# Strassen's algorithm for the down projection of three of four token tiles, in an attention and gated feed-forward kernel

## The chip, the cores and the metric

The kernel runs on one core of a Trainium2 chip. Its time is the device time of one execution in microseconds; the number given for a kernel is the median over several executions. A profiled execution has a time of its own and a span, from its first to its last instruction, that is a little shorter.

The engines are named as in the profile: PE (TensorE, matrix products into PSUM, the accumulation memory), PEld (PE's weight loads), DVE (VectorE), ACT (ScalarE), POOL (GpSimd, which can't read PSUM) and SP (SyncE, which issues the DMAs here). Each engine works through its own queue strictly in order.

## The reference

For x of 2048 tokens and D = 512, with 32 heads of 16 and a window of 256 keys:

```python
xn  = layernorm(x)
q, k, v = heads(xn @ wqkv)                       # 32 heads of 16
p   = softmax(mask(q @ k.T * 16 ** -0.5))        # causal, 256 keys back
s   = (p @ v) @ wo
h   = silu(xn @ w1) * (xn @ w3)                  # F = 1792
g   = silu(h @ w2)                               # the down projection
out = x + s * g
```

Everything is float32 at the interface. The down projection multiplies h (2048 x 1792) by w2 (1792 x 512).

## The kernel before

**Precision.** Operands of the large products are split into two float16 parts, hi and lo, and a product is three passes: hi x hi, hi x lo, lo x hi. A cast on ACT makes hi (`slot<-slot` on line 947 for h), and a subtraction makes lo: on POOL, by `halves` (line 325), which does every 512 columns as two instructions of 256.

**Tiling.** Tokens are worked on in NT = 4 tiles of TW = 512. Attention for a tile goes by 4 groups of 8 heads and 2 halves of a group, so there are 32 `units`. In a unit, `pass2` makes scores (line 717), adds masks on DVE (line 724), takes the exponential on ACT (line 727: four per unit in the first tile, five in the others, 152 in all) and multiplies by the values (line 745); `pass1` finds the maxima two units ahead (lines 637 and 651). Scores have two PSUM buffers. `normalise` ends a group of heads: the sums of the exponentials go by DMA through `dd`, `dr`, `de` to `rb`, POOL multiplies `on` by `rb`, ACT copies to hi (line 799), and POOL subtracts for lo. These are the operands of the output projection, `total`.

**Feed-forward.** F is cut into FB = 14 blocks of 128. `gate_up(t, f)` makes the gate and up products of a block (24 passes of 512 columns, line 918), tanh on ACT (line 933), two products on DVE (lines 937 and 942), then hi and lo of h. `down(t, k, b)` multiplies for one of four groups of blocks (`GROUPS`: 4, 4, 3 and 3 blocks) and one of four blocks `b` of 128 tokens: h is the stationary operand and w2 the moving one, 512 columns wide, three passes a block (line 968). A group's sum is brought out of PSUM with its scale, `down_scale[k]`, by ACT for the first group (line 987, tiles after the first) and by DVE for the others (line 992), which adds to an accumulator `ACC[t, b]`. `total(t, b)` takes tanh of it, multiplies O by wo (line 1019), and combines (line 1023); the last block of the last tile goes by columns (`total_by_columns`, 256 wide, line 1048). These dense products alternate between two PSUM banks, `m0` and `m1`.

**Weights.** In the first tile `measure`, `measure_down` and their `cut` scale and split w1, w3 and w2; the split forms are stored to DRAM (`dW1`, `dW2`) and loaded again by `load` and `load_down` in the other tiles. wo is cut at the start of the second tile.

**Order.** PE's order is written out by the program. `feed_forward` lists the dense pieces with costs in passes; `spread` puts each unit's share of them between the batches of attention, so that every unit is of like length; `later(n, f)` issues f n steps on. What is left of the dense list when attention ends (84 passes are kept back, `KEEP`) and the last tile's `total` follow at the end without attention. For ACT, DVE, POOL and SP a list scheduler orders the instructions by when it takes them to be ready; `urgent` raises priority. The order is fixed when the kernel is built.

**Slots.** Most tiles of 2 KB a partition come from a ring of SLOTS = 40 slots (`take`, `give`), taken in the order in which they were given back.

## Time and profile before

| | us |
|---|---|
| median of 3 executions | 824.92 (824.75 to 825.98) |
| the profiled execution | 823.93 |
| its span | 822.1 |
| PE busy in it | 802.3 |
| DVE, ACT, POOL busy | 633.5, 389.4, 205.9 |

A group's row reads: line, engine, operation, result<-operands, their shape, xcount | busy us, mean ns of one | us that the engine was idle just before them, and what ended most of that. Matrix passes are pipelined: one has a modelled length of 379 ns at 512 columns while the next starts after 216, so lengths from start to start are read from rows that merge several. A row of the chain reads: start us, us, what. A row of waits reads: who waited for whom, us in total, times, longest. A row of a timeline reads: start us, us, engine, line, operation, and in brackets the idle time before it.

### The profile page before, as it was taken

The page shows a single profiled execution, that of the slowest core. Times are in us where ns is not written, and L with a number is a line of the kernel's source. Part 1 is how long each engine was busy: PE and PEld are TensorE (multiplying, and loading weights), DVE is VectorE, ACT ScalarE, POOL GpSimd, SP SyncE. Part 2 cuts the span into 40 slices and gives each one's busy share as a digit, 9 for nine tenths or more (in the row PEclk, how much of TensorE's full clock was granted, in tenths as well). Part 3 has the DMA queues.
Part 4 walks back from the last instruction along what each step waited for, and adds up shares of the span by engine and source line. Part 5 has one row for each costly group of instructions (what it writes and reads, how often), then busy time and mean ns, then how long its engine had stood idle before and what let it go on. Part 6 is the DMA issues. An engine that isn't in the chain of part 4 may idle for free. (4 is left out here: it accounts for less than half of the span.)

```text
span 822.1 us, 22902 instructions
## 1 busy us (share of the span) xinstructions
PE 802.3 (98%) x8924; PEld 380.1 (46%) x8924; DVE 633.5 (77%) x2021; ACT 389.4 (47%) x562; POOL 205.9 (25%) x355
## 2 busy tenths in 40 slices
PE   8999999999999999999999999999999999999998
PEld 4444444444444444444445444444444444444444
DVE  8787788888787588878878876877777787776435
ACT  6889785645345344243343444442433344432511
POOL 2237274342203113021211112120202022030301
PEclk9999999999999999999999999999999999999999
DMA  9987656157442444544434334534434343332101
GB/s 283 251 252 236 208 176 203 63 148 242 126 134 78 120 131 126 153 124 134 136 94 131 99 89 144 136 121 121 129 82 143 105 112 116 108 121 86 52 22 53
DMA packets 95326, 110.66 MB, mean 135 GB/s; under 512 B 17200, under 2 KB 60528, under 8 KB 95216
## 3 DMA queue, kind: packets, MB, share of 16 engines
q1 hardware_dynamic: 94928, 108.67, 45.3%
q8 instruction: 70, 1.15, 0.6%
q10 hardware_dynamic: 288, 0.52, 0.2%
q14 instruction: 40, 0.33, 0.1%
HBM read 76.28 MB, written 28.57 MB: 128 GB/s over the span
## 5 line engine op out<-in xcount | busy, mean ns | idle before, releaser
L325 POOL TENSOR_TENSOR slot<-slot,slot 128x256 f16<-128x256 f32 (+1 forms) x228 | 151.5, 691 | 518.5 <-ACT slot L947 391.9
L918 PE MATMUL m<-XH,slot 128*128 128x512 f16 x896 | 267.3, 380 | 3.1 <-DVE slot L937 1.7
L727 ACT ACTIVATE pt<-s,es 128x1024 f32<-128x1024 f32 x152 | 167.7, 1113 | 194.4 <-DVE s L724 192.5
L918 PEld LDWEIGHTS <-slot 128*128 128x128 f16 x1344 | 125.1, 98 | 158.1 <-issue 14.0
L918 PE MATMUL m<-XL,slot 128*128 128x512 f16 x448 | 169.8, 379 | 0.0
L968 PE MATMUL m<-slot,slot 128*128 128x512 f16 x672 | 156.6, 380 | 1.8 <-DVE slot L594 0.7
L724 DVE TENSOR_TENSOR s<-s,MK 128x256 f32<-128x256 f32 (+2 forms) x280 | 118.4, 435 | 49.5 <-PE s L717 47.1
L651 DVE CUSTOM_DVE_ANT_0 junk<-s,MW 128x320 bf16<-128x320 f32 x276 | 134.1, 486 | 24.3 <-PE s L637 15.8
L968 PEld LDWEIGHTS <-slot 128*128 128x128 f16 x672 | 61.9, 98 | 80.4 <-issue 9.9
L651 DVE CUSTOM_DVE_ANT_0 junk<-po,MW 128x320 bf16<-128x320 f32 x172 | 83.6, 486 | 5.1 <-DVE mt L676 0.3
L745 PE MATMUL po<-pt,V 64*32 64x320 f32 (+4 forms) x2880 | 77.2, 342 | 0.0
L947 ACT CAST slot<-slot 128x512 f16<-128x512 f32 x56 | 34.5, 617 | 73.4 <-DVE slot L942 68.7
L933 ACT ACTIVATE slot<-m,sgs 128x512 f32<-128x512 f32 x56 | 38.3, 684 | 56.8 <-PE m L918 56.8
L745 PEld LDWEIGHTS po<-pt,V 64*32 64x32 f32 x2880 | 51.0, 106 | 21.4 <-issue 0.8
L717 PE MATMUL s<-qa,KA 50*64 50x320 f16 (+3 forms) x1472 | 58.2, 259 | 1.2 <-ACT pt L727 0.6
L937 DVE SCALAR_TENSOR_TENSOR slot<-slot,m 128x512 f32<-128x512 f32 x56 | 38.3, 685 | 23.4 <-ACT slot L933 23.2
L717 PEld LDWEIGHTS <-KA 50*64 50x64 f16 x1472 | 30.2, 105 | 55.6 <-issue 34.0
L637 PE MATMUL s<-KA,qa 48*64 48x320 f16 (+3 forms) x824 | 45.4, 294 | 2.9 <-ACT pt L727 1.6
L942 DVE SCALAR_TENSOR_TENSOR slot<-m,slot 128x512 f32<-128x512 f32 x56 | 38.5, 688 | 10.6 <-PE m L918 10.1
L992 DVE SCALAR_TENSOR_TENSOR slot<-m,dsc,slot 128x512 f32<-128x512 f32 x48 | 35.9, 748 | 13.4 <-PE m L968 13.1
L581 PE MATMUL m<-XH,whi 128*128 128x512 f16 x120 | 44.7, 381 | 1.1 <-DVE slot L937 0.7
L581 PE MATMUL m<-XL,whi 128*128 128x512 f16 x120 | 44.5, 379 | 0.0
(162 smaller groups left out, 875.2 us busy)
## 6 DMA issues: line engine op xcount, KB each, us to landing
slot<-dW SPq DMA_DIRECT2D x126, 256.0 KB
slot<-in_B_w_dram SPq DMA_DIRECT2D x42, 256.0 KB
dW<-slot SPq DMA_DIRECT2D x42, 256.0 KB
slot<-in_A_x_dram SPq DMA_DIRECT2D x30, 256.0 KB
KA<-dK SPq DMA_DIRECT2D x24, 288.0 KB
qa<-dQ SPq DMA_DIRECT2D x32, 192.0 KB
dQ<-slot SPq DMA_DIRECT2D x16, 256.0 KB
dK<-slot SPq DMA_DIRECT2D x16, 256.0 KB
```

Source lines behind the costliest of these rows:

```text
L325: op(out[:, c], a[:, c], b[:, c])
L581: nc.tensor.matmul(cell["pp"], a[:, k, c, :], b[:, c, :], start=(c, i) == parts[0][0], stop=(c, i) == parts[-1][-1])
L637: nc.tensor.matmul(s[c:c + w, r, :n], qa[rows, 2 * p + a, ii * P + c:ii * P + c + w], ka[rows, 2 * p + a, e - n:e], start=True, stop=True)
L651: lasts["maximum"] = nc.vector.tensor_tensor_reduce(out=junk[:, :n], in0=s[:, r, :n], in1=mask, scale=1.0, scalar=NEG, op0=ALU.add, op1=AL ...
L717: nc.tensor.matmul(s[64 * h:64 * h + 64, r, o:o + 64 * n], ka[rows, 2 * p + a, 64 * (m + 4):64 * (m + 5)], qa[rows, 2 * p + a, 64 * (m + k ...
L724: nc.vector.tensor_add(v, v, MK[:, kind, of:of + n, :].unsqueeze(1).to_broadcast([P, 2 * len(which), n, 64]))
L727: nc.scalar.activation(pt, s, AF.Exp, scale=es)
L745: nc.tensor.matmul(cell["po"][32 * i:32 * i + 32, h, 64 * (m + k):64 * (m + k + n)], V[64 * h:64 * h + 64, (4 * t + m // 2) % VB, hd * VW: ...
L918: nc.tensor.matmul(cell[k], w[:, (a * NC + c) * P:(a * NC + c + 1) * P], b[:, c, :], start=c == 0 and i == 0, stop=c == NC - 1 and i == 2)
L933: nc.scalar.activation(sg, cell[0], AF.Tanh, scale=sg_scale[:, f:f + 1])
L942: lasts["emptied"] = nc.vector.scalar_tensor_tensor(sg, cell[1], 0.5 * HS / (WS * XS)**2, sg, op0=ALU.mult, op1=ALU.mult)
L968: nc.tensor.matmul(ps, hh[:, a * TW + b * P:a * TW + (b + 1) * P], w[:, c * D:(c + 1) * D], start=f == f0 and i == 0, stop=f == f1 - 1 and ...
```

## The change

In the first tile nothing but where things go changes: `down` is as before, and the split w2 isn't stored. In the second to fourth tile the down projection goes by Strassen's algorithm in Winograd's form. The 14 blocks of F are taken as 7 pairs, an even and an odd block. The even and odd block and the even and odd 128 tokens make four blocks of h; the two blocks of w2 and the left and right 256 columns of D make four blocks of w2. Seven products of sums of these, each 256 columns wide, take the place of eight, and each is again three passes. The pairs are in two parts (`FOLDS`: 4 and 3 pairs), so that a product is summed over 4 or 3 pairs in PSUM, twice for the two halves of its tokens.

- `fold_weights(j)`, in the second tile, after its blocks 1 to 7: loads a pair of rows of w2 again, scales them on ACT (one scale for all, from `fold_scales`), makes four sums on POOL, casts all four tiles on ACT, subtracts on POOL, and stores seven operands to DRAM.
- `fold_first` and `fold_second`, after an even and an odd block: the same for h, with four sums on POOL.
- `folds`, `load_fold`, `fold_down_piece`: the loads (two products ahead) and the products, in the order `SEVEN`; the first part is brought out of PSUM by ACT, the second added by DVE.
- `unfold`: 14 additions of 256 columns on POOL turn the seven results into the four accumulators.
- 47 slots instead of 40 and a smaller scratch for DMA descriptors; the last unit's `negate` at once; the last tile's output blocks in the order 1, 3, 0, 2.

```diff
-SLOTS = 40
+SLOTS = 47
+FOLDS = ((0, 4), (4, 7))
+SEVEN = (0, 1, 3, 4, 5, 6, 2)
...
-    dW2 = dram.tile([FB, P, 2 * D], F16, name="dW2")
+    dW2 = dram.tile([7, P, FB // 2, D], F16, name="dW2")
...
-                later(2, negate)
+                later(2, negate) if (t, g, p) != units[-1] else negate()
...
+    def fold_weights(j):
+
+        raws = [take(F32) for _ in range(2)]
+        for i, raw in enumerate(raws):
+            nc.sync.dma_start(raw, w2[(2 * j + i) * P:(2 * j + i + 1) * P, :])
+        e, o = raws
+        l, r = slice(0, 256), slice(256, 512)
+        sub = nc.gpsimd.tensor_sub
+        cell = {}
+
+        def sums():
+            assert folded
+            for i, raw in enumerate(raws):
+                nc.scalar.activation(raw, raw, AF.Copy, scale=fold_w[:, 2 * j + i:2 * j + i + 1])
+            cell["z"] = z, y = [take(F32) for _ in range(2)]
+            pool_parts(sub, (z[:, l], e[:, r], e[:, l]), (z[:, r], o[:, r], z[:, l]),
+                       (y[:, l], o[:, r], e[:, r]), (y[:, r], o[:, l], z[:, r]))
+
+        def cut(raw, n, which):
+
+            a = take(F16)
+            nc.scalar.copy(a[:, 0:n], raw[:, 0:n])
+            for c in range(0, n, 256):
+                sub(a[:, n + c:n + c + 256], raw[:, c:c + 256], a[:, c:c + 256])
+            give(raw, after=4)
...
+        later(4, sums)
+        later(6, lambda: cut(e, 256, (0,)))
+        later(7, lambda: cut(o, 512, (1, 2)))
+        later(9, lambda: cut(cell["z"][0], 512, (4, 5)))
+        later(11, lambda: cut(cell["z"][1], 512, (6, 3)))
...
+    def fold_second(t, j):
...
+        nc.gpsimd.tensor_add(z[:, 0], ee[:, 1], oo[:, 1])
+        sub(z[:, 1], z[:, 0], ee[:, 0])
+        sub(y[:, 0], ee[:, 0], ee[:, 1])
+        sub(y[:, 1], oo[:, 0], z[:, 1])
+        cut(o, oo, (1, 3), (e,))
+        later(1, lambda: cut(sums[0], z, (4, 5)))
+        later(2, lambda: cut(sums[1], y, (6, 2)))
...
+    def fold_down_piece(t, k, i):
...
+            for j in range(j0, j1):
+                made, lo, at = AS[t, j, i]
+                wj = w[(j - j0) // 2][:, (j - j0) % 2 * D:]
+                for n, (a, b) in enumerate(((0, 0), (0, 1), (1, 0))):
+                    f = at + a * lo + c * P
+                    nc.tensor.matmul(ps, made[:, f:f + P], wj[:, 256 * b:256 * b + 256],
+                                     start=j == j0 and n == 0, stop=j == j1 - 1 and n == 2)
...
+            if k == 0:
+                QS7[t, i] = take(F32)
+                with urgent():
+                    nc.scalar.activation(QS7[t, i], ps, AF.Copy, scale=fold_down)
+                return
+            q = QS7[t, i]
+            with urgent():
+                lasts["emptied"] = nc.vector.scalar_tensor_tensor(q, ps, fold_down, q, op0=ALU.mult, op1=ALU.add)
+            if i != SEVEN[-1]:
+                return
+            unfold(t)
...
+    def unfold(t):
...
+        halves(add, q[5], q[5], q[0])
+        halves(add, q[6], q[6], q[5])
+        into(1, 0, q[6], q[3])
+        into(1, 1, q[6], q[4])
+        into(0, 0, q[0], q[1])
+        halves(add, q[5], q[5], q[4])
+        into(0, 1, q[5], q[2])
...
+                    if t == 1 and 1 <= f <= FB // 2:
+                        pieces.append((0, lambda f=f: fold_weights(f - 1)))
...
+                if f == 0 and t > 1:
+                    pieces += soon
...
+                for k, (j0, j1) in enumerate(FOLDS):
+                    if t and f == 2 * j1 - 1:
+                        soon, late = folds(t, k)
+                        if k == 0 or t == NT - 1:
+                            pieces += soon
...
-    for b in range(4):
-        if b < 2:
-            residual(NT - 1, b + 2)
-        if b < 3:
-            run(total(NT - 1, b))
-    total_by_columns(NT - 1, 3)
+    for n, b in enumerate((1, 3, 0)):
+        if n < 2:
+            residual(NT - 1, 2 * n)
+        run(total(NT - 1, b))
+    total_by_columns(NT - 1, 2)
...
-    nc = _bacc.Bacc("TRN2", target_bir_lowering=False, num_devices=1)
+    nc = _bacc.Bacc("TRN2", target_bir_lowering=False, num_devices=1, dynamic_dma_scratch_size=1024)
```

The products of a part follow the gate and up products of the next block, as the groups did before; those of a tile's second part fall into the next tile's first block, and in the last tile they come at the end.

More of the change, by code (lines that the diff above doesn't have):

```diff
@@ L859, in tile_block, with load_down @@
     NORMS = {}
[L861 to L865 removed]
+    def load_down(f):
         RAW2[f] = raw = take(F32)
@@ new lines, in fold_second, with cut @@
+    def fold_second(t, j):
+        e, o = (HH.pop((t, 2 * j + i)) for i in range(2))
+        ee, oo = by_parity(e), by_parity(o)
+        sub = nc.gpsimd.tensor_sub
+        sums = [take(F32) for _ in range(2)]
+        z, y = (a.rearrange("p (e c q) -> p e c q", c=2, e=2) for a in sums)
+        def cut(raw, view, which, give_too=()):
+            made = take(F16)
+            hi, lo = (made[:, 512 * k:512 * k + 512].rearrange("p (e c q) -> p e c q", e=2, c=2) for k in range(2))
+            nc.scalar.copy(hi, view)
+            for k in range(2):
+                sub(lo[:, k], view[:, k], hi[:, k])
+            for k, i in enumerate(which):
+                operand(t, j, i, made, 512, 256 * k)
+            give(raw, *give_too, after=4)
+        nc.gpsimd.tensor_add(z[:, 0], ee[:, 1], oo[:, 1])
[5 more added lines that the diff above has]
+        later(2, lambda: cut(sums[1], y, (6, 2)))
@@ new lines, in unfold, with into @@
+    def unfold(t):
+        q = [QS7.pop((t, i)) for i in range(7)]
+        add = nc.gpsimd.tensor_add
+        for b in range(4):
+            ACC[t, b] = take(F32)
+        def into(e, d, x, y):
+            for c in range(2):
+                h = slice(256 * c, 256 * c + 256)
+                add(ACC[t, 2 * c + e][:, 256 * d:256 * d + 256], x[:, h], y[:, h])
+        halves(add, q[5], q[5], q[0])
[5 more added lines that the diff above has]
+        into(0, 1, q[5], q[2])
+        give(*q, after=6)
+        summed.update((t, b) for b in range(4))
@@ L953, in tile_block, with folds @@
+    def folds(t, k):
+        loads = [(0, lambda i=i: load_fold(t, k, i)) for i in SEVEN]
+        pieces = []
+        for n, i in enumerate(SEVEN):
+            if n + 2 < 7:
+                pieces.append(loads[n + 2])
+            pieces += fold_down_piece(t, k, i)
+        return loads[:2], pieces
     ACC = {}
@@ L970, in part @@
                 if b == 3:
-                    give(hh)
-                    if t == 0:
-                        def store(f=f, w=w):
-                            nc.sync.dma_start(dW2[f], w)
-                            give(w, after=3)
-                        later(4, store)
-                    else:
-                        give(w)
+                    give(hh, w)
             if fs[-1] < f1 - 1:
@@ L1318, in tile_block @@
             later(1, lambda k=k: fetch(*tiles[k]))
-    for b in range(2):
+    for b in (1, 3):
         residual(NT - 1, b)
```

90 lines of the change are left out of this document (80 added, 10 removed).

## The prediction

> **What bounds the kernel now.** I read the page's shares first, then the groups by line with the shapes kept apart, the waits of PE, and last the end of the span in order of time.
>
> ```profile
> span 822.1 us, 22902 instructions
> PE 802.3 (98%) x8924; PEld 380.1 (46%) x8924; DVE 633.5 (77%) x2021; ACT 389.4 (47%) x562; POOL 205.9 (25%) x355
> PE   8999999999999999999999999999999999999998
> POOL 2237274342203113021211112120202022030301
> PEclk9999999999999999999999999999999999999999
> ```
>
> PE is busy nearly everywhere at full clock; no other engine reaches 80%. A busy PE could still hide stalls, so I look at what one pass costs from start to start and at what PE waits for.
>
> ```profile
> PE s L670 <- DVE NM L664: 1.8, 3, 1.1
> PE m L918 <- DVE slot L937: 1.7, 3, 0.8
> PE s L637 <- ACT pt L727: 1.6, 4, 0.7
> ```
>
> ```profile
> 808.12 7.77 PE m L1019 x36
> 815.89 2.63 PE m L1048 x24
> ```
>
> The longest sum of PE's waits on one cause is 1.8 us, so time taken from PE's own work comes off the span as long as nobody else becomes late. From the chain: 36 passes of 512 columns take 7.77 us, 0.2158 us each, and 24 passes of 256 columns 2.63 us, 0.1096 us each. A pass of half the width costs half.
>
> **The change, part by part.**
>
> *PE.* Tiles two to four lose 3 x 14 x 4 x 3 = 504 passes of 512 columns (of the 672 below) and gain 3 tiles x 7 products x 7 pairs of blocks x 2 halves x 3 terms = 882 passes of 256.
>
> ```profile
> L968 PE MATMUL m<-slot,slot 128*128 128x512 f16 x672 | 156.6, 380 | 1.8 <-DVE slot L594 0.7 <-DVE slot L942 0.5 <-POOL slot L325 0.2
> L1048 PE MATMUL m<-slot,slot 128*128 128x256 f16 x24 | 2.8, 272 | 0.0
> ```
>
> 504 x 0.2158 = 108.8 us go, 882 x 0.1096 = 96.7 us come: **-12.1 us**. The second row has a fresh weight load before every half-width pass, as the new products have, so the price includes it.
>
> *Work for POOL.* It replaces the two casts' differences of a pair of blocks (4 instructions of 256 columns) by 11, for 21 pairs; adds 11 for each of 7 pairs of rows of w2 in the second tile; and 14 for each tile's sums at the end. 292 instructions of 128x256 become 558.
>
> ```profile
> L325 POOL TENSOR_TENSOR slot<-slot,slot 128x256 f16<-128x256 f32 x204 | 134.0, 685 | 468.8 <-ACT slot L947 391.9 <-ACT slot L329 52.2 <-DMA slot<-in_B_w_dram 7.3
> L325 POOL TENSOR_TENSOR on<-on,rb 128x256 f32<-128x256 f32 x32 | 22.7, 732 | 62.6 <-DMA rb<-de 62.6
> L325 POOL TENSOR_TENSOR slot<-on,slot 128x256 f16<-128x256 f32 x32 | 20.8, 672 | 14.6 <-ACT slot L799 14.6
> L325 POOL TENSOR_TENSOR slot<-slot,slot 128x256 f32<-128x256 f32 x24 | 17.4, 747 | 49.7 <-DVE slot L1023 41.8 <-issue 7.9
> ```
>
> Over the whole span this is about 558 x 0.70 = 391 us, under half of it, and would hide. It isn't spread evenly. The built order of the changed kernel has a stretch in the second tile in which w2 is combined, its first four pairs are combined, and wo is cut, all at once. Take two marks that both kernels share, the exponentials, which ScalarE takes in the same order: between the 31st and the 45th of the 152, POOL must do 110 instructions (73 to f16, 37 to f32), the last of them before the 45th, because ScalarE's queue holds a copy of POOL's result ahead of it; the first of the 110 needs a copy queued behind the 31st. Before, these two exponentials stand here:
>
> ```profile
> 237.34 1.11 ACT L727 ACTIVATE pt<-s,es 128x1024 f32<-128x1024 f32 x1 [2.37 <-DVE s L724]
> 238.35 0.68 ACT L933 ACTIVATE slot<-m,sgs 128x512 f32<-128x512 f32 x1
> ...
> 306.60 1.11 ACT L727 ACTIVATE pt<-s,es 128x1024 f32<-128x1024 f32 x1 [0.55 <-DVE s L724]
> ```
>
> ```profile
> 239.00:306.60 67.60, 67.18 (x806) 32.22 (x805) 50.56 (x166) 31.91 (x43) 15.37 (x23) 1.00 0.40 113
> ```
>
> The window row (PE, PEld, DVE, ACT, POOL busy, clock, DMA share, GB/s) shows POOL with 23 instructions and 15.4 us in these 68 us. From 239.0 to 305.3 (306.6 less the copy and a hand-over) there are 66.3 us; the work is 73 x 0.685 + 37 x 0.747 = 77.6 us. So POOL is 11.3 us late at the 45th exponential, and late already at the 41st. Behind a late copy on ScalarE stand the exponentials and the tanh of gate blocks; behind the tanh, the products on VectorE; behind these PE's banks. What slack has an exponential? 14 of them in 69.3 us is 4.95 us each; the mask additions and the exponential take 2 x 0.43 + 1.11 of it.
>
> ```profile
> L724 DVE TENSOR_TENSOR s<-s,MK 128x256 f32<-128x256 f32 x224 | 92.3, 427 | 47.1 <-PE s L717 45.4 <-PE s L670 1.0
> L947 ACT CAST slot<-slot 128x512 f16<-128x512 f32 x56 | 34.5, 617 | 73.4 <-DVE slot L942 68.7 <-issue 2.2 <-DMA on<-os 1.9
> L328 ACT ACTIVATE slot<-slot,sw 128x512 f32<-128x512 f32 x14 | 9.8, 720 | 3.5 <-DVE sw L894 3.5
> L987 ACT ACTIVATE slot<-m,dsc 128x512 f32<-128x512 f32 x12 | 8.2, 685 | 8.9 <-PE m L968 8.9
> L992 DVE SCALAR_TENSOR_TENSOR slot<-m,dsc,slot 128x512 f32<-128x512 f32 x48 | 35.9, 748 | 13.4 <-PE m L968 13.1
> ```
>
> About 2.5 us are left over before PE wants the score bank again, so PE loses about 9. ScalarE itself has 81 instructions there instead of 43, roughly 13 x 1.11 + 68 x 0.61 = 56 of the 66 us, so two nearly full queues wait for each other; I add 1. **+10 us**, estimate from these rows; bounds 0 (POOL catches up) and 18 (POOL begins one exponential later, 4 us, and stands for the DMA of rb as long as before on average, 62.6/16 = 3.9 us).
>
> The GPSIMD Engine Reference of the Trainium skill (section 3.1) gives 2.6 cycles per element at 1.2 GHz for two-input elementwise work, 0.555 us for 256 columns without dispatch, as an estimate. By it the 110 would take 61 us, POOL would be in time, and the sum below would be 821.5. The rows of 0.685 and 0.747 stand against it.
>
> *Drains and casts.* In each tile 12 drains on VectorE (0.748) become 7, and 4 on ScalarE (0.685) become 7; the pairs get four casts instead of two, one of half width. VectorE gains 15 x 0.75 = 11 us of idle time, worth nothing while PE has the span. ScalarE at 47% covers its part, except in the stretch above.
>
> *DMA and SP's queue.* 42 loads of dW2 become 84 (half products, 256 or 128 KB), 14 stores become 49 of 128 KB, and w2 is read a second time (14 x 256 KB). In the stretch this adds 6.4 + 3.7 = 10.1 MB to 113 GB/s x 80 us = 9 MB: the DMA share goes from 0.40 to about 0.85, still under full. On SP a store that waits for a late POOL holds back the gate weights behind it; these are issued two blocks ahead, some 18 us, which covers 11. Price 0; if the lag passed 18 us, its excess.
>
> *Slots, scratch, the last unit's negation, the order of the residuals.* Space and order; two VectorE instructions of under 0.4 us move earlier. Nothing.
>
> *The end.* Here is the old one:
>
> ```profile
> 799.55 8.56 PE L968 MATMUL m<-slot,slot 128*128 128x512 f16 x36
> 807.95 7.93 PE L1019 MATMUL m<-slot,slot 128*128 128x512 f16 x36
> ...
> 808.49 0.74 DVE L992 SCALAR_TENSOR_TENSOR slot<-m,dsc,slot 128x512 f32<-128x512 f32 x1
> ...
> 807.75 0.60 ACT L799 CAST slot<-on 128x512 f16<-128x512 f32 x1
> ...
> 802.43 1.42 POOL L325 TENSOR_TENSOR on<-on,rb 128x256 f32<-128x256 f32 x2
> 808.43 1.30 POOL L325 TENSOR_TENSOR slot<-on,slot 128x256 f16<-128x256 f32 x2 [4.58 <-ACT slot L799]
> ```
>
> The last head group's output is normalised (on x rb), copied and cut for wo, just in time for the first block of L1019. In the built order of the changed kernel POOL has on x rb behind all 14 sums of the last tile, and its copy on ScalarE stands behind the four tanh that wait for these sums. Call E the moment PE ends the last product. A drain ends 1.28 us after its last pass (807.95 to 809.23); the product before the last ends at E - 1.96 (18 x 0.109), its drain at E - 0.7. Then 10 sums, 10 x 0.72 = 7.2: E + 6.5; on x rb 1.42: E + 7.9; copy 0.6 and hand-overs: E + 8.6; the first difference 0.65: E + 9.3. PE comes to these operands after 9 of 12 passes, at E + 1.94, and ends the block near E + 9.5 instead of E + 2.6: **+6.9 us**. What follows (three more blocks, last drain, store) shifts as it is. PE then stood still for 6.7 us. The only start from rest in this trace is the first:
>
> ```profile
> L1216 PE MATMUL m<-onesb 128*128 128x512 bf16 x10 | 4.2, 598 | 1.0 <-DVE onesb L189 1.0
> ...
> L1216 PE MATMUL m<-onesb 128*128 128x512 bf16 x16 | 3.8, 392 | 0.0
> ```
>
> (first 1 to 5 us, then 5 to 8 us): 10 passes in the first 4 us where 10 x 0.216 would do, 1.8 us lost. I take **+1.8** after the pause; bounds 0 and 1.8.
>
> **Sum.** 822.1 - 12.1 + 10 + 6.9 + 1.8 = 828.7 us span. The profiled execution took 823.93, 1.8 more than its span, and lies 1.0 under the median of 824.92: 831.5 us.
>
> **The rivals.**
>
> *POOL keeps pace in the second tile* (ends on the other side). It decides at 0.625 us for one POOL instruction (66.3 + 2.5 us over 110), or if PE reaches the score banks later than I think. For it: POOL was idle for three quarters of that stretch before, and VectorE's work, beside which these rows were taken, gets less. Against it: no row is under 0.67. Time 831.5 - 10 = 821.5.
>
> *Two full queues block each other.* POOL waits for copies that stand behind exponentials that wait for PE that waits for ScalarE: the upper bound, 18 instead of 10: 839.5. For it: ScalarE's 56 of 66 us. Against: POOL's order was laid down with its load in it.
>
> *The whole gain arrives:* no lag, and on x rb is in time after all: 822.1 - 12.1 + 2.8 = 812.8. Against it: the order of an engine's queue isn't a matter of speed.
>
> *Half-width passes don't cost half,* because each carries a weight load (98 ns each) that no longer fits behind it: 882 x (0.1096 + 0.098) against 504 x (0.2158 + 0.098), +25 us, 850 or more. Against it: the 24 passes of 0.1096 us carry such loads too. TensorE: Matmul & The Clock Gate of the Trainium skill (section Back-to-back issue gap) has a figure that points the same way, 81 ns a pass at 128 columns and 131 at 512 in a stream with weight loads; by it the products would cost, as an estimate, at least 882 x 0.081 = 71 us against 504 x 0.131 = 66. This trace disagrees: its passes of 512 columns take 0.2158 us.
>
> ```profile
> L968 PEld LDWEIGHTS <-slot 128*128 128x128 f16 x672 | 61.9, 98 | 80.4 <-issue 9.9
> ```
>
> **How the numbers follow.** Forecast 0.46 (its own range 826 to 836), blocked queues 0.25, POOL in pace 0.20, whole gain 0.07, dear passes 0.02. Within 0.2% (1.6 us, about what can be told from no change) falls a quarter of POOL in pace and a little of the forecast's low end: 0.06. Faster 0.15 + 0.07 = 0.22, slower 0.72. The range 819 to 843 leaves out the whole gain, the dear passes, the best of POOL in pace and the worst of the blocked queues, less than 0.2 together.
>
> **What would show it.** Right: in the products' row, 882 passes of 256 columns near 0.11 us apart; between the 31st and 45th exponential POOL busy almost without a break, the distance of the two 78 to 85 us instead of 69, ScalarE's idle time there put down to POOL; at the end PE standing 6 to 7 us within the first output block, released by POOL, and then some passes 0.43 us apart. Wrong: the two exponentials under 71 us apart; PE's pause at the end under 3 us; or a new wait elsewhere, for instance PE for a load of dW2 (two products ahead, in the last tile 1.96 us each) or POOL's 10.5 us of sums holding up on x rb at the start of the third and fourth tile.

## The result and the profile after

| | before | changed |
|---|---|---|
| median of 6 executions each, us | 825.08 (824.72 to 826.38) | 891.23 (888.39 to 895.36) |
| the profiled execution, its span | 823.93, 822.1 | 890.93, 889.2 |

The changed kernel takes 1.080 times as long (95% interval 1.0776 to 1.0828): 66 us slower, where the prediction had 6.6 us and at most 18.

The page of the changed kernel: span, busy time by engine, then PE, POOL and PE's granted clock in the 40 slices of the span (22 us each).

```profile
span 889.2 us, 24220 instructions
PE 812.9 (91%) x9302; PEld 424.7 (48%) x9302; DVE 629.3 (71%) x2013; ACT 434.3 (49%) x655; POOL 384.1 (43%) x621
PE   8999988999889669999999999999999998989995
POOL 2257353524278786113351635310434453441653
PEclk9999999999989779999999999999999998999997
```

No engine is full: PE fell from 98% to 91%, and POOL, with nearly twice its old time, is at 43%. PE's digits are lowest in the 14th and 15th slice (the second tile) and in the last one; fainter losses are in the 6th, 7th, 11th, 12th, 34th and 36th. PE's longest waits, and those of ScalarE (ACT) that the new work makes:

```profile
PE s L719 <- ACT pt L729: 18.6, 8, 5.8
PE m L978 <- DVE slot L997: 13.6, 5, 7.4
PE s L639 <- ACT pt L729: 10.8, 10, 2.7
PE m L1212 <- ACT slot L801: 7.3, 1, 7.3
```

```profile
ACT slot L801 <- POOL on L327: 36.6, 13, 6.7
ACT slot L1055 <- POOL slot L1063: 22.0, 20, 2.1
ACT slot L1206 <- POOL slot L1132: 19.2, 3, 12.3
ACT slot L1055 <- POOL slot L1065: 10.1, 16, 0.7
```

L729 is the exponential, L719 and L639 the score products that need its PSUM bank, L978 the gate and up products, L1212 the output projection. L1055 is a cast of a pair of blocks of h, L1062 to L1065 are POOL's four sums before it, L925 the sums of w2, L1206 the tanh ahead of `total`, L1132 sums of `unfold`. PE waits for exponentials, ScalarE for POOL; in the kernel before, PE's waits on one cause came to 1.8 us at most. Of the three waits at L1206, one of 4.6 us is at the start of the fourth tile, and the other two, 14.6 us, come after the last exponential.

The 152 exponentials are the same in every kernel here, in the same order, so their starts (rows of L729 in the timeline) say where time is lost. In us later than in the kernel before:

| up to exponential | 23 | 31 | 45 | 61 | 109 | 139 | 152 | PE's end |
|---|---|---|---|---|---|---|---|---|
| changed kernel | 5.8 | 7.5 | 37.1 | 39.2 | 43.2 | 61.0 | 59.0 | 66.9 |

So 29.6 us are lost in the second tile between the 31st and the 45th, 17.8 late in attention (109 to 139), 7.9 at the end, 7.5 before the 31st. In the second tile exponentials stand whose scores are ready: from the end of their masks to their start, the 14 from the 32nd to the 45th stand at least 36.1 us in all, against 3.1 before. The second tile in windows of 20 us (busy us and instructions of PE, PEld, DVE, ACT and POOL, then clock, DMA share, GB/s):

```profile
260.00:280.00 20.00, 16.40 (x147) 7.46 (x147) 12.81 (x40) 11.83 (x19) 17.86 (x28) 0.83 0.43 122
280.00:300.00 20.00, 12.62 (x163) 5.60 (x161) 9.51 (x28) 9.49 (x14) 16.11 (x25) 0.81 0.50 137
300.00:320.00 20.00, 14.23 (x103) 6.06 (x102) 9.51 (x32) 8.85 (x14) 14.14 (x23) 0.76 0.54 155
320.00:340.00 20.00, 16.67 (x193) 8.41 (x192) 10.87 (x32) 10.07 (x15) 12.43 (x19) 0.91 0.76 226
```

POOL is busy for 60.5 of these 80 us, ScalarE for 40, PE for 60: they take turns at waiting. The chain of work that ended last shows how, in order of time:

```profile
301.74 0.59 SPq L769
...
303.01 0.54 SPq L770
...
303.64 2.67 DMA slot<-in_B_w_dram
...
306.34 0.73 ACT slot L940
...
307.14 2.09 POOL slot L925 x3
...
315.89 2.51 POOL slot L1057 x4
...
320.68 1.27 POOL slot L1057 x2
...
323.74 2.01 ACT pt L729 x2
```

SyncE (SP) sends a load of w2 late, behind other transfers; ScalarE's scaling (L940) stands for it and POOL's sums for the scaling. POOL then works without a break to 321.95, and two casts and a scaling on ScalarE later come two exponentials. And at the end:

```profile
871.55 1.82 POOL on L327 x2
873.37 0.02 issue
873.39 0.63 ACT slot L801
874.02 0.05 issue
874.06 8.70 PE m L1212 x27
882.76 2.63 PE m L1241 x24
```

The multiplication by rb comes behind the unfolding's sums, its copy behind that, and PE stands 7.3 us; then 27 passes take 8.70 us instead of 27 x 0.2158 = 5.83.

### The profile page after: what moved, and what is told of

Same layout as the page of the kernel before. It is cut to its first block, busy times and chain, and to the rows that moved or that the text cites. A ratio compares the mean times of both kernels' runs of the same rounds, so it can differ in the third digit from the quotient of the medians.

```text
span 889.2 us, 24220 instructions
## 1 busy us (share of the span) xinstructions
PE 812.9 (91%) x9302; PEld 424.7 (48%) x9302; DVE 629.3 (71%) x2013; ACT 434.3 (49%) x655; POOL 384.1 (43%) x621
## 4 chain that ended last, share of the span: by engine, by line
PE 53%; DVE 12%; POOL 11%; ACT 10%; DMA 6%; issue 5%; SPq 2%; ACTq 0%; POOLq 0%; DVEq 0%
PE m L978 17%; PE m L1098 8%; PE po L747 7%; PE m L1212 5%; PE m L583 4%; DVE junk L653 3%; PE s L719 3%; PE m L553 3%; DMA slot<-in_B_w_dram 3%; POOL slot L327 3%; ACT pt L729 2%; ACT slot L330 2%; POOL slot L1057 2%; PE s L639 2%; DVE s L726 2%
## 5 line engine op out<-in xcount | busy, mean ns | idle before, releaser
L978 PE MATMUL m<-XH,slot 128*128 128x512 f16 x896 | 272.8, 387 | 17.5 <-DVE slot L997 13.6
L729 ACT ACTIVATE pt<-s,es 128x1024 f32<-128x1024 f32 x152 | 167.3, 1110 | 152.7 <-DVE s L726 145.3
L978 PEld LDWEIGHTS <-slot 128*128 128x128 f16 x1344 | 126.3, 99 | 178.0 <-issue 38.1
L327 POOL TENSOR_TENSOR slot<-slot,slot 128x256 f16<-128x256 f32 (+1 forms) x162 | 108.2, 695 | 195.5 <-ACT slot L1011 60.5
L978 PE MATMUL m<-XL,slot 128*128 128x512 f16 x448 | 172.3, 385 | 0.0
L1098 PE MATMUL m<-slot,slot 128*128 128x256 f16 x882 | 102.5, 273 | 1.4 <-DVE slot L596 1.1
L1098 PEld LDWEIGHTS <-slot 128*128 128x128 f16 x882 | 84.5, 98 | 18.2 <-issue 4.6
L1057 POOL TENSOR_TENSOR slot<-slot,slot 128x256 f16<-128x256 f32 x126 | 82.0, 679 | 0.0
L719 PE MATMUL s<-qa,KA 50*64 50x320 f16 (+3 forms) x1472 | 60.6, 263 | 22.9 <-ACT pt L729 18.6
L1055 ACT CAST slot<-slot 128x512 f16<-128x512 f32 x63 | 38.9, 617 | 64.1 <-DVE slot L1002 31.8
L719 PEld LDWEIGHTS <-KA 50*64 50x64 f16 x1472 | 32.0, 106 | 74.8 <-issue 52.7
L1062 POOL TENSOR_TENSOR slot<-slot,slot 128x256 f32<-128x256 f32 x21 | 15.3, 727 | 99.2 <-DVE slot L1002 99.2
L639 PE MATMUL s<-KA,qa 48*64 48x320 f16 (+3 forms) x824 | 46.2, 297 | 12.1 <-ACT pt L729 10.8
L1212 PE MATMUL m<-slot,slot 128*128 128x512 f16 x180 | 47.8, 415 | 7.9 <-ACT slot L801 7.3
L327 POOL TENSOR_TENSOR on<-on,rb 128x256 f32<-128x256 f32 x32 | 23.1, 741 | 59.3 <-DMA rb<-de 59.2
```

The costliest lines, as they stand in the source:

```text
L327: op(out[:, c], a[:, c], b[:, c])
L639: nc.tensor.matmul(s[c:c + w, r, :n], qa[rows, 2 * p + a, ii * P + c:ii * P + c + w], ka[rows, 2 * p + a, e - n:e], start=True, stop=True)
L719: nc.tensor.matmul(s[64 * h:64 * h + 64, r, o:o + 64 * n], ka[rows, 2 * p + a, 64 * (m + 4):64 * (m + 5)], qa[rows, 2 * p + a, 64 * (m + k ...
L729: nc.scalar.activation(pt, s, AF.Exp, scale=es)
L978: nc.tensor.matmul(cell[k], w[:, (a * NC + c) * P:(a * NC + c + 1) * P], b[:, c, :], start=c == 0 and i == 0, stop=c == NC - 1 and i == 2)
L1055: nc.scalar.copy(hi, view)
```

## The experiments

The theory that came out of this: lateness reaches PE through queues that are worked off in order. An instruction on ScalarE (or a DMA on SyncE) that waits for POOL or for a load holds up the exponential behind it, and PE waits for that. The rivals: POOL has too much work; the smaller passes don't pay; the slots or the DMAs are the cause. All times are medians; ratios are to runs of the kernel before beside them (825.1 to 826.0 us).

### Leaving work out

**The end.** The last group's multiplication and cut go ahead of most of the last tile's sums.

```diff
-        later(26, cut)
+        later(26 if (t, g) != (NT - 1, NG - 1) else 13, cut)
...
         halves(add, q[5], q[5], q[0])
+        into(0, 0, q[0], q[1])
+        with tc.issue_after(lasts["normal"].ins) if t == NT - 1 else nullcontext():
             halves(add, q[6], q[6], q[5])
```

> The last head group's on x rb, its copy and its cut are put ahead of the last tile's sums in POOL's order; the result is the same. Theory (POOL's order makes PE wait at the end): PE's pause of 7.3 us for the copy of on goes, and with it the 13 passes at half clock, 2.7 us; a pause under 1.5 us stays; 891 becomes 880 to 883. Rival (the sums themselves are late, the tanh of the first block takes the wait over): at most 3 us go, 888 to 891.

889.87 us, ratio 1.0769 (1.0736 to 1.0802): the rival's range. The median is 1.4 us less, no more than the runs scatter; in the traces, 3.0 us less from the last exponential to PE's end. The wait moved: in the waits of this kernel PE now stands for DVE, which finishes an output block that waited for the tanh of the late sums.

```profile
PE m L1214 <- DVE slot L1218: 4.7, 1, 4.7
```

**w2's sums.** POOL's 11 instructions for each pair of rows of w2 are left out; loads, casts and stores stay.

```diff
-            cell["z"] = z, y = [take(F32) for _ in range(2)]
-            pool_parts(sub, (z[:, l], e[:, r], e[:, l]), (z[:, r], o[:, r], z[:, l]),
-                       (y[:, l], o[:, r], e[:, r]), (y[:, r], o[:, l], z[:, r]))
...
-            for c in range(0, n, 256):
-                sub(a[:, n + c:n + c + 256], raw[:, c:c + 256], a[:, c:c + 256])
```

> Leaves out POOL's whole part in combining w2 (four sums and seven subtractions for each of 7 pairs of rows); the casts, the loads and the stores stay, the stores write hi twice. Theory (POOL is overloaded in the second tile, and ScalarE, VectorE and PE wait in turn): the distance of the 31st and 45th exponential comes back from 99 us to under 75, 891 becomes 850 to 862. Rival (SP's queue and the DMAs of the second reading and the stores are what is late): those are all still there, 885 to 891.

871.95 us, ratio 1.0564 (1.0527 to 1.06): 19 us less, not the 29 to 41 expected. The 31st and 45th exponential are 83.1 us apart (98.9 in the changed kernel, 69.3 before): half of what the second tile lost isn't POOL's combining of w2.

**The pairs' sums.** The four sums of a pair are left out, the casts read the blocks themselves.

```diff
-        nc.gpsimd.tensor_add(z[:, 0], ee[:, 1], oo[:, 1])
-        sub(z[:, 1], z[:, 0], ee[:, 0])
-        sub(y[:, 0], ee[:, 0], ee[:, 1])
-        sub(y[:, 1], oo[:, 0], z[:, 1])
```

> Leaves out the four sums of each pair of blocks of h on POOL; the casts on ScalarE read the two blocks as they are, so no cast waits for POOL; the casts and the subtractions stay. Theory (in every pair ScalarE's queue stands for POOL's short chain of sums, and exponentials behind it come late): the third and fourth tile give back 12 to 20 us, the second, where POOL has 28 instructions less, 5 to 10 more: 862 to 874. Rival (only the overload of the second tile counts): 3 to 8 us in that tile alone, 883 to 888.

865.08 us, ratio 1.0479 (1.0459 to 1.05): 26 us less, within the theory's range, from 3 us of POOL's work for each of 21 pairs. The 139th exponential is 35.5 us late instead of 61; 13.6 of these 25.5 us come between the 109th and the 139th, 5.5 before the 31st.

**All three.**

> The three edits together: combining w2 and the pairs' sums are left out, the end is in order. Theory (the passes save 12 us, and all that was lost is POOL's): 811 to 820. Rival (slots, loads of the half products or dearer passes lose part of it too): 825 to 850.

847.27 us, ratio 1.0277 (1.0251 to 1.0303): the rival's range, 34 us above what the passes alone should give. A part of what is left stands in the timeline of this kernel at the start of the third tile (POOL, then ScalarE):

```profile
459.35 1.42 POOL L327 TENSOR_TENSOR on<-on,rb 128x256 f32<-128x256 f32 x2 [12.77 <-DMA slot<-dW]
...
470.08 1.40 POOL L1124 TENSOR_TENSOR slot<-slot,slot 128x256 f32<-128x256 f32 x2
...
471.50 0.63 ACT L1199 ACTIVATE slot<-slot 128x512 f32<-128x512 f32 x1 [9.57 <-POOL slot L1124]
472.04 1.10 ACT L729 ACTIVATE pt<-s,es 128x1024 f32<-128x1024 f32 x1
```

POOL stands 12.8 us for a DMA, the unfolding's sums are behind it, the tanh of the total waits 9.6 us for them, and the exponential, whose scores were ready, comes after that tanh. Hence the next four.

**Slots alone** (the kernel before with 47 slots and the smaller scratch):

```diff
-SLOTS = 40
+SLOTS = 47
```

> The kernel before with 47 slots instead of 40 and the smaller DMA scratch, and nothing else of the change. Theory (what the change costs is work that holds up ScalarE's and SyncE's queues, and the slots by themselves cost nothing, as the prediction had it): 824 to 827 us. Rival (the changed kernel is already 6 us late by its 31st exponential, in the first tile's part of the run, where it does little that is new; the round of 47 slots moves the loads of w2 in the first tile and that is the cause): 828 to 832 us, with the 31st exponential 3 to 6 us later than before.

826.45 us, ratio 1.0005 (0.9996 to 1.0015), the theory's range. In the kernel before, the slots cost nothing.

**The unfolding's sums, too; the second reading of w2, too; both.**

```diff
         for b in range(4):
-            ACC[t, b] = take(F32)
+            ACC[t, b] = q[b]
...
-        halves(add, q[5], q[5], q[0])
-        halves(add, q[6], q[6], q[5])
-        into(1, 0, q[6], q[3])
-        into(1, 1, q[6], q[4])
-        into(0, 0, q[0], q[1])
-        halves(add, q[5], q[5], q[4])
-        into(0, 1, q[5], q[2])
```

```diff
-                    if t == 1 and 1 <= f <= FB // 2:
-                        pieces.append((0, lambda f=f: fold_weights(f - 1)))
```

> The kernel that leaves out all three (847.3 us: no combining of w2 at POOL, no sums of the pairs, the last group's multiplication ahead), and it leaves out the 14 sums of a tile that turn seven products into four blocks, too: the first four products stand for the blocks. Theory (the sums stand at POOL behind the on x rb that waits for its DMA, ScalarE's tanh of the total waits for them and exponentials stand behind that tanh: about 9 us at the start of the third tile, 2 at that of the fourth, 3 to 6 at the end): 829 to 837 us, and the pause of 5.3 us at the start of the third tile is gone. Rival (the tanh is only the last of several that come late there; on x rb itself takes the place): 841 to 847 us.

> The kernel that leaves out all three (847.3 us), and it leaves out the second reading of w2 in the second tile, too (14 loads, 14 scalings and 28 casts at ScalarE, 49 stores); what the products read is written in the first tile from the parts that are there, in 14 stores. Theory (ScalarE's scalings wait for those loads, which come late from SyncE's queue, and the casts stand ahead of exponentials and tanh: 10 us between the 31st and the 49th exponential): 834 to 840 us, the 31st and the 49th exponential 60 to 63 us less than 5 us later than in the kernel before. Rival (the loss there is the late start of the products' operands of the second tile, whatever w2 does): 844 to 848 us.

> Leaves out all of it: the combining and second reading of w2, the sums of the pairs and the 14 sums of the unfolding; the last group's multiplication stands ahead. What is left of the change is 882 passes of 256 columns instead of 504 of 512, their operands' casts, drains and loads. Theory (the costs add up and the passes give what the sum said, 12 us): 813 to 822 us. Rival (the passes of 256 columns, or the casts that they need, give less than the sum said): 825 to 832 us.

835.99 (ratio 1.0124, 1.0109 to 1.0139), 839.05 (1.0158, 1.0141 to 1.0175) and 825.21 us (0.999, 0.998 to 1.0). The unfolding is worth 11.3 us, the second reading 8.2, and both 22.1. Between the 77th and the 85th exponential, about the pause shown above, the kernel without the unfolding needs 42.2 us instead of 49.8, and from the 152nd to PE's end 35.3 instead of 42.9. It gives back 6.7 us up to the 49th exponential, and up to there the five engines' queues hold the same instructions in the same order in both kernels; what makes it isn't known. So a difference of a few us between two versions here isn't by itself the worth of what was edited; it counts where it also stands at the place of the edit. The second reading shows between the 31st and the 45th exponential: 68.4 us apart instead of 79.6. But the time with both out is the rival's, not the 813 to 822 of the passes' 12 us; in the first tile this kernel is 9.2 us late at the 23rd exponential, behind a load of w2 that waited in SyncE's queue. Its 14 substitute stores are my own doing, so they went next.

```diff
-            nc.sync.dma_start(made[-1].rearrange("p (j d) -> p j d", d=D)[:, 0:n], dW2[i, :, j:j + n, :])
+            nc.sync.dma_start(made[-1][:, 0:n * D], dW1[i, j % 2][:, 0:n * D])
```

> As the kernel that leaves out all of it (825.2 us), and without the 14 stores of the first tile that stood in for those of the second reading: the products' weights are read from where the first tile puts w1 and w3, so they are not w2's. Theory (the passes of 256 columns give the 10 to 12 us that the sum said from the 23rd exponential on, and what hid them was a pause of 5.1 us in the first tile, behind a load of w2 that SyncE sent late because of those stores): 817 to 821 us, the 23rd exponential at most 5 us late instead of 9. Rival (the pause comes from the round of slots in the first tile whatever is stored): 823 to 827 us.

820.82 us, ratio 0.9948 (0.993 to 0.9966). This is about the ceiling of this form: without the sums and the second reading that the seven products need, the change brings 4.6 us. The 23rd exponential is still 6.6 us late, more than the 5 expected; from there to PE's end this kernel gains 8.6 us. So passes of half the width do pay. Each counted to the start of PE's next instruction, pauses included, the 882 new passes take 100.2 us in this trace and the 504 old ones of tiles two to four 115.0 in the kernel before: 14.8 us less, no worse than the 12.1 of the sum. Some 6 us of that are lost elsewhere, and where wasn't found.

### Keeping the work, changing the order

To leave work out takes away both the work and the waiting. These keep all of it. First, the casts of a pair's sums four and six steps later, and each sum of the unfolding as soon as its products are there:

```diff
-        later(1, lambda: cut(sums[0], z, (4, 5)))
-        later(2, lambda: cut(sums[1], y, (6, 2)))
+        later(4, lambda: cut(sums[0], z, (4, 5)))
+        later(6, lambda: cut(sums[1], y, (6, 2)))
```

> The whole of the changed kernel, with the same work in another order: the casts of a pair's two sums stand four and six steps behind the pair instead of one and two, the sums of the unfolding are made as soon as their products are there (two stand behind the last product instead of 14), and the last group's cut stands 13 steps earlier. Theory (what the sums of the pairs and of the unfolding cost is ScalarE standing in its queue for POOL; with the same work behind its due time it waits for nothing): 858 to 872 us, of the 891 us, with ScalarE's waits for POOL at the casts of the pairs under 10 us instead of 32. Rival (POOL is so late that its work itself is what comes late, wherever ScalarE stands): 880 to 893 us.

893.82 us, ratio 1.0838 (1.0814 to 1.0861). That looks like the rival, but ScalarE's order is the same as before: each of the 63 casts of pairs stands behind as many exponentials as in the changed kernel, and ScalarE's waits for POOL at them are 33 us (23.8 + 9.4), not under 10. The list scheduler put them where it had them before, though they were asked for later. The experiment hadn't changed what it meant to. With the same order, the second tile by the plain product and w2 combined over its 14 blocks:

```diff
-                    if t == 1 and 1 <= f <= FB // 2:
-                        pieces.append((0, lambda f=f: fold_weights(f - 1)))
+                    if t == 1:
+                        pieces.append((0, lambda t=t, f=f: load_down(t, f)))
+                        if f % 2 == 1:
+                            pieces.append((0, lambda f=f: fold_weights(f // 2)))
...
-                    if t and f == 2 * j1 - 1:
+                    if t > 1 and f == 2 * j1 - 1:
```

> As the one with the other order, and the second tile is projected by the plain product of the kernel before (14 stores in the first tile, 14 loads in the second), so that the seven products serve the third and fourth tile alone and w2 is combined over all 14 blocks of the second tile instead of 7. The passes would give two thirds: about 7 us. Theory (POOL and ScalarE have room for the combining where it is spread over 145 us instead of 70): 820 to 832 us. Rival (the second reading and its casts hold up ScalarE's queue wherever they stand): 838 to 855 us.

859.24 us, ratio 1.0395 (1.0364 to 1.0427), above both ranges. Now an order that the scheduler has to keep. In the changed kernel the two casts of a pair's sums go behind the newest exponential; they are also asked for three and six steps later instead of one and two, which by itself moved none of them above.

```diff
+                lasts["exp"] = nc.scalar.activation(pt, s, AF.Exp, scale=es)
...
+            with tc.issue_after(lasts["exp"].ins) if raw is not o else nullcontext():
                 nc.scalar.copy(hi, view)
...
-        later(1, lambda: cut(sums[0], z, (4, 5)))
-        later(2, lambda: cut(sums[1], y, (6, 2)))
+        last = (t, j) == (NT - 1, FB // 2 - 1)
+        later(1 if last else 3, lambda: cut(sums[0], z, (4, 5)))
+        later(2 if last else 6, lambda: cut(sums[1], y, (6, 2)))
```

> The whole of the changed kernel; only the two casts of a pair's sums are put behind the newest exponential in ScalarE's queue by an order that the planner has to keep (in the run with the other order the planner had put them back where they were). Theory (ScalarE stands 1 us in front of each cast for POOL's sum while an exponential behind it could run): 870 to 881 us, ScalarE's waits for POOL at these casts under 12 us instead of 32, the stall of PE between the 109th and the 139th exponential under 8 us instead of 15. Rival (the 26 us that leaving out the sums gave are POOL's own lateness, not ScalarE's order): 886 to 895 us.

875.56 us, ratio 1.0589 (1.0563 to 1.0615): 15.7 us for the same work in another order (24,213 instructions in its trace, 24,220 in the changed kernel's). The gain is where the changed kernel lost 17.8 us: between the 109th and the 139th exponential it is 4.4 now. In the second tile nothing is gained, the 31st and 45th are 101.5 us apart. Here is one pair, in the timeline of the changed kernel (scores' mask on DVE, then ScalarE, then POOL):

```profile
520.18 0.69 DVE L726 TENSOR_TENSOR s<-s,MK 128x512 f32<-128x512 f32 x1
...
520.29 0.62 ACT L1055 CAST slot<-slot 128x512 f16<-128x512 f32 x1 [4.81 <-DVE slot L1002]
521.91 0.62 ACT L1055 CAST slot<-slot 128x512 f16<-128x512 f32 x1 [0.99 <-POOL slot L1063]
522.43 1.11 ACT L729 ACTIVATE pt<-s,es 128x1024 f32<-128x1024 f32 x1
...
521.15 0.73 POOL L1063 TENSOR_TENSOR slot<-slot,slot 128x256 f32<-128x256 f32 x1
```

and in that of the kernel with the casts behind:

```profile
519.32 0.69 DVE L726 TENSOR_TENSOR s<-s,MK 128x512 f32<-128x512 f32 x1
...
519.43 0.62 ACT L1056 CAST slot<-slot 128x512 f16<-128x512 f32 x1 [4.80 <-DVE slot L1002]
520.10 1.11 ACT L729 ACTIVATE pt<-s,es 128x1024 f32<-128x1024 f32 x1
521.11 0.61 ACT L1056 CAST slot<-slot 128x512 f16<-128x512 f32 x1
```

The scores are ready at 520.87, and the exponential starts at 522.43, because a cast in front of it waits 0.99 us for POOL and then takes its own time; in the other order it starts 0.09 us after the scores. ScalarE's wait at these casts fell from 22.0 + 10.1 us to

```profile
ACT slot L1056 <- POOL slot L1064: 8.4, 6, 3.0
...
ACT slot L1056 <- POOL slot L1066: 0.7, 1, 0.7
```

Then the same for the scalings and casts of w2, which also stand a few steps later, as do the stores:

```diff
+            with tc.issue_after(lasts["exp"].ins):
                 for i, raw in enumerate(raws):
                     nc.scalar.activation(raw, raw, AF.Copy, scale=fold_w[:, 2 * j + i:2 * j + i + 1])
...
-        later(4, sums)
+        later(6, sums)
...
-            later(4, store)
+            later(8, store)
```

> As the one with the pairs' casts behind the exponentials, and the scalings and casts of the second reading of w2 stand behind the newest exponential, too, two to four steps later, its stores four steps later. Theory (the same mechanism makes most of the 19 and the 8 us of w2): 850 to 866 us, the distance of the 31st and the 45th exponential under 85 us instead of 98.9. Rival (POOL's 11 sums for each pair of blocks are too many for that stretch whatever the order): the distance stays over 92 us and the time over 866 us.

862.61 us, ratio 1.0442 (1.0425 to 1.046). The 31st and 45th exponential are 86.4 us apart, 15 less than in the run before and a little over the 85 expected, with all 11 instructions of POOL for each pair of rows. But the deadline now bites: PE waits for the products' weights themselves, and by the 61st exponential the kernel is 33.1 us late.

```profile
PE m L1102 <- DMA slot<-dW: 7.6, 1, 7.6
PE m L1216 <- ACT slot L801: 7.3, 1, 7.3
```

Next, POOL's order: the multiplication by rb later and behind the newest sums of an unfolding, and at the end the last group's ahead (as in the first experiment).

```diff
-            halves(nc.gpsimd.tensor_mul, on, on, rb)
+        def mul():
+            with tc.issue_after(lasts["unfold"].ins) if "unfold" in lasts else nullcontext():
+                halves(nc.gpsimd.tensor_mul, on, on, rb)
...
+        later(12 if last else 20, mul)
```

> As the one before it, and POOL multiplies on by rb eight steps later, behind the newest sums of an unfolding, and at the end the last group's multiplication and cut stand ahead of the last ten sums of the unfolding. All of the work is there. Theory: 838 to 856 us. Rival (the start of the third and of the fourth tile are not held up by that order, and at the end the wait only moves, as it did before): within 4 us of the one before it.

857.8 us, ratio 1.0387 (1.0364 to 1.0411): a little above the range, 4.8 us less than the one before. From the 61st to the 152nd exponential this kernel loses nothing (30.1 us late at the one, 28.9 at the other), but neither does the one before it (33.1 and 31.8): at the start of the third and fourth tile the new order of POOL is worth nothing, as the rival had it. At the end it is worth 4.5 us, from the last exponential to PE's end (45.4 to 40.9). What is left is the second tile and 3.8 us at the end. So, last, the second tile by the plain product, w2 combined over its 14 blocks, with all these orders:

> All of the work in the order of the run before it (857.8 us), and the second tile is projected by the plain product, so that w2 is combined over its 14 blocks and the seven products serve the third and fourth tile. Theory (of the 32 us that the run before it is still above the kernel before, 29 are made in the second tile by the combining of w2, now as late loads of the products' weights; over 14 blocks and without their deadline it is hidden): 824 to 838 us, the 61st exponential at most 10 us later than in the kernel before instead of 30. Rival (the second reading costs PE's path what it costs wherever it is spread): 842 to 856 us.

838.41 us, ratio 1.0147 (1.0131 to 1.0164), 0.4 us above the theory's range. The 61st exponential is 8.8 us late instead of 30.1. Three things change in the second tile at once: the products' weights have no deadline there, w2 is combined at half the rate, and the tile's own pairs are gone. Which of them gave the 21 us isn't shown. From the page:

```profile
span 839.2 us, 23914 instructions
PE 804.1 (96%) x9176; PEld 407.4 (49%) x9176; DVE 630.8 (75%) x2018; ACT 423.4 (50%) x638; POOL 342.7 (41%) x558
PEclk9999999999999999899999999999999999999998
```

It is the best version with all of the work: 20.8 us under the version of the same shape without the orders, 53 under the changed kernel, and still 1.5% slower than the kernel before. No version with all of the work was found that beats that kernel; the barest, with work left out, is only 0.5% under it.

## Why the prediction was wrong, step by step

- **Drains and casts** (worth nothing; "ScalarE at 47% covers its part, except in the stretch above"): this step failed, and with the next it carries the error. It went by ScalarE's share of busy time. A cast that waits 1 us for POOL costs ScalarE no busy time, but everything behind it stands. Leaving out the sums of the pairs gave 26 us, and 15.7 us come back by the order of their casts alone. PSUM — Partial Sum Buffer of the Trainium skill (section Engine vs sequencer instructions) says that ScalarE's queue is strictly first in, first out; the pair above agrees, 1.56 us behind ready scores.
- **Work for POOL in the second tile** (+10, bounds 0 to 18): the place was right to the exponential, the size was not: 29.6 us. And the reason was half right. The work was foreseen well: between these two exponentials POOL does 114 instructions, 79.1 us by their rows (110 and 77.6 in the prediction). But the step took it that POOL then works almost without a break, and POOL is busy for only 74.6 of the 98.9 us: it waits as well. With all of that work kept, another order at ScalarE brought the distance from 101.5 to 86.4. POOL's part in combining w2 accounts for 15.8 us of the distance (98.9 to 83.1), the second reading of w2, priced at nothing, for 11.2 more (79.6 to 68.4, both without POOL's sums). The rival of two queues that block each other was the nearest, but its 8 us on top were bounded by one exponential and one wait.
- **DMA and SP's queue** (price 0; "some 18 us, which covers 11"): the second reading is worth 8.2 us, together with its scalings and casts on ScalarE, which the experiment left out, too. The lead was that of gate weights; the loads of w2 itself, which ScalarE's scalings wait for, had none to spare in the chain above.
- **Start of the third and fourth tile:** named only as what could go wrong (14 sums in front of the multiplication by rb), and not priced. Where a pause was found, with POOL's other work left out, it came the other way round: the sums stand behind the multiplication, which waits for its DMA, and that cost 7.6 us at the start of the third tile. In the changed kernel itself the same stretch is 3.2 us longer than before (44.1 against 40.9), and a wait of 4.6 us for the sums stands at the start of the fourth tile.
- **The end** (+6.9 and +1.8): 7.3 us of pause and 8.70 - 5.83 = 2.9 us of half-speed passes. Right. But it isn't worth that much: with that wait taken away 1.4 us are gained (3.0 by the traces), since the tanh of the same sums is next.
- **PE** (-12.1): right for the passes themselves (14.8 us less, counted from start to start), though the barest version keeps only 8.6 of it from the 23rd exponential on. Passes of half the width aren't dear: in the changed kernel their row has 273 ns, the old one 272.

```profile
L1098 PE MATMUL m<-slot,slot 128*128 128x256 f16 x882 | 102.5, 273 | 1.4 <-DVE slot L596 1.1 <-POOL slot L1057 0.2
```

- **Slots** (nothing): right, by the experiment with slots alone. The changed kernel's 5.8 us up to the 23rd exponential, before any of the new sums, weren't priced and weren't settled: slots alone give 2.0, the last version, with stores of w2's parts in that tile, 1.8, and the one with larger substitute stores 9.2.
- **POOL in pace** (821.5), a rival, needed 0.625 us for an instruction; the sums of w2 took 0.728. The GPSIMD Engine Reference of the Trainium skill (section 3.1) gives 2.6 cycles per element at 1.2 GHz for two inputs, 0.555 us for 256 columns as an estimate; the trace disagrees again.

```profile
L925 POOL TENSOR_TENSOR slot<-slot,slot 128x256 f32<-128x256 f32 x21 | 14.9, 728 | 13.1 <-DMA dK<-slot 9.8 <-PE m L978 1.8 <-ACT slot L940 1.2
```

In short: the sum priced each place by the work that doesn't fit there. What cost time was for a good part that work which does fit waits in front of work on the critical path: with all of the work kept, order alone brought back 33 of the 66 us (857.8). The rest, nearly all of it in the second tile, went only with another shape of that tile, and its cause stays in part open.

## What to carry to other kernels

When a change gives an idle engine work whose result a busy queue picks up, price the wait at each pick-up (here 1.1 us on average at 20 of 21 first casts, and 0.6 at 16 of the second), not the idle engine's total. Where the order is a scheduler's, asking for an instruction later may change nothing, as here; an order that it must keep moved it. An experiment on order has to show first that the order changed. And before a trade of passes for sums, measure the ceiling with the sums left out: here 4.6 us, for 66 to be risked.

## What else the runs showed of the hardware

- PE's pauses cost more than their length when long. In the changed kernel each of the five pauses over 4 us (from start to start) was followed by 6 to 13 passes of 512 columns some 0.43 us apart instead of 0.216, the one of 3.6 us by 4, and most of the shorter ones by none. In all 68 such passes stand in its trace, 4 in that of the kernel before; at 0.21 us too much each this is, as an estimate, some 14 of the 66 us. TensorE: Matmul & The Clock Gate of the Trainium skill (section What's actually happening) has half clock after an idle window of about 3.4 us. The pauses agree for the greater part, but 13 slow passes also followed two of 2.2 and 1.4 us in quick succession, and 7 followed one of 1.8 us.
- At the end of the changed kernel, three pairs of 256-column instructions on POOL in a row, two of additions and the multiplication by rb, took 1.85 to 1.86 us each where such a pair takes 1.40 to 1.42 elsewhere (the rows of 459 and 470 us above). The cause wasn't tried.
- SyncE sends DMAs one at a time, 0.54 to 0.59 us each in the chain at 301 to 303 us of the changed kernel (two are shown above). By the line that issues them, the medians in this trace run from 0.25 to 0.58 us.
